# Attention with a gated MLP on one core: block 3 of the attention weights is copied to an fp32r tile, and its four transposes take fp32r operands

## The chip, the cores and the metric

The kernel runs on one core of a Trainium2 chip. The metric is the device time of one execution in microseconds. Before the change it is 828.13 us, the median of three runs (826.8 to 829.23).

## The reference

Eight batches with eight heads, 576 tokens, head size 64. For each head a causal attention with an extra bias from a running sum of `s`; the concatenated heads are the input `x` of a gated MLP that also mixes tokens. All in fp32.

```python
scores = scale * np.matmul(q, k.transpose(0, 1, 3, 2))
cum = np.cumsum(np.maximum(s, 0.0), axis=-1)
bias = -(cum[:, :, :, None] - cum[:, :, None, :])
scores = np.where(causal, -1000000000.0, scores + np.minimum(bias, 0.0))
attn = np.exp(scores - np.max(scores, axis=-1, keepdims=True))
attn = attn / (np.sum(attn, axis=-1, keepdims=True) + 1e-09)
o = np.matmul(attn, v)                       # then x = heads side by side
h = gelu(x @ w_in); u, v = halves of h
v_s = einsum('ts,bsd->btd', w_sg, layernorm(v) * g_ln) + b_sg
out = x + (u * v_s) @ w_out
```

## The kernel before

There are 64 heads (8 batches of 8), and after each 8 heads the MLP of that batch. A list of steps with due times (`POS`, in units of a head) sets the order in which the code issues them, with the MLP of batch b spread over the eight heads that come after it; a scheduler then orders the instructions of each engine from that list, and every engine runs its own list strictly in order. SyncE (SP) issues all transfers, from one queue.

**Precision.** Heads 0 to 7 use fp32 for scores, heads 0 to 11 for the product with the values (`NQ = 8`, `NP = 12`). From there on, operands are split in two fp32r tiles, a rounded part (hi) and the rest (lo), and a product is made of several fp32r matmuls that add up. In the code fp32r tiles are `F32R`; the profile prints fp32 and fp32r operands of a matmul alike as f32.

**A head**, in four generators that are advanced in turn:

- `split_head` splits keys and queries into `k1`, `k2`, and copies parts of them with transfers to `q1`, `q2` and back (L281 to L285).
- `scores` makes the scores of five blocks of query rows, `it` 0 to 4. Block 3 has 128 rows and 448 keys (`ITW`), block 0 has 64 rows and 64 keys. For each block VectorE adds the mask and takes the minimum of the negated scores (L305), which writes the block to `p`, ScalarE takes the exponential in place (L315). When all five are there, `norm` takes the reciprocals of the sums, and GpSimd multiplies each block in place (L338). Block 0 is not kept by itself: its normalised 64x64 values are written into columns 384 to 447, rows 0 to 63 of block 3, whose tile is 512 columns wide (`PW`). In the same way the second part of block 1 goes into block 2. So there are six operations on GpSimd per head from head 12 on. The `p` tiles exist twice (`pbuf`, by head parity), so a block of head h+2 can be written once block h has been read.
- `transposes` turns the blocks so that the keys stand on partitions: 13 transposes of 128x128 (one of them 64 columns) in four groups, each group in one bank of PSUM. A transpose is a matmul with the block's 128 columns as the loaded weights and the identity matrix `ident` as the moving operand (L377). Block 3 has four of the 13: columns 0 to 127 in the first group, 128 to 383 in the second, 384 to 511 in the fourth. After each group ScalarE and VectorE split the bank into hi and lo.
- `pv` multiplies with the values.

Weights, masks and the identity are made or loaded at the start, on VectorE and GpSimd, beside the running sums of `s`.

Of the kernel before, what the change touches and what calls it, by code (L numbers as in the profile page):

```python
# [8 lines left out]
F32 = mybir.dt.float32  # L9
F32R = mybir.dt.float32r  # L10
# [10 lines left out]
P = 128  # L21
# [16 lines left out]
PW = [64, 192, 384, 512, 576]  # L38
# [9 lines left out]
NP = 12  # L48
# [11 lines left out]
def tile_attn_gmlp(  # L60
# [12 lines left out]
    nc = tc.nc  # L73

    const = ctx.enter_context(tc.tile_pool(name="const", bufs=1))
    att = ctx.enter_context(tc.tile_pool(name="att", bufs=2))
# [6 lines left out]
    def eng(key):  # L83
        return [{"s": nc.scalar, "g": nc.gpsimd, "v": nc.vector}[x] for x in ENG[key]]

    def split(hi, lo, src, eng_hi, eng_lo):
        if eng_hi is nc.scalar:
            nc.scalar.copy(out=hi, in_=src)  # L88
        elif eng_hi is nc.gpsimd:
            nc.gpsimd.tensor_scalar(out=hi, in0=src, scalar1=1.0, scalar2=1.0, op0=ALU.mult, op1=ALU.mult)  # L90
        else:
            nc.vector.tensor_copy(out=hi, in_=src)
        eng_lo.tensor_tensor(out=lo, in0=src, in1=hi.bitcast(F32), op=ALU.subtract)  # L93

    heads = {}
# [41 lines left out]
    for c0, n in ((0, 512), (512, REM)):  # L137
        ps = ps_sc.tile([P, 512], F32, name="cps", tag="sc")
# [10 lines left out]
    for i in range(WARM):  # L149
# [7 lines left out]
    ident = const.tile([P, P], F32, name="ident")  # L157
    nc.vector.memset(ident, 0.0)
    nc.gpsimd.affine_select(out=ident, in_=ident, pattern=[[1, P]], base=0, channel_multiplier=-1,
                            compare_op=ALU.not_equal, fill=1.0)  # L160
    mask = const.tile([P, 448], BF16, name="mask")
    nc.vector.memset(mask, 0.0)
    nc.gpsimd.affine_select(out=mask, in_=mask, pattern=[[-1, 448]], base=320, channel_multiplier=1,
# [12 lines left out]
    pbuf = []  # L176
# [141 lines left out]
    def norm(h, its, rs):  # L318
        c = slice(min(its), max(its) + 1)
        nc.scalar.activation(out=rs[:, c], in_=sums[h % 2][:, c], func=AF.Copy, bias=1e-9)  # L320
        nc.vector.reciprocal(out=rs[:, c], in_=rs[:, c])  # L321
        for it in its:
            r, w = ITR[it], ITW[it]
            p = pbuf[h % 2][it][0:r, 0:w]
            e = eng("n0" if h < NP else "n")[it]


            o = [(p, p, rs[0:r, it:it + 1])]
            if it == 0:
                o = [(pbuf[h % 2][3][0:64, 384:448], p, rs[0:64, 0:1])]  # L330
            elif it == 1:
                o = [(p[:, 0:P], p[:, 0:P], rs[:, 1:2]),
                     (pbuf[h % 2][2][64:P, 256:320], p[64:P, P:192], rs[64:P, 1:2])]
            for po, pi, f in o:
                if e is nc.scalar:
                    nc.scalar.activation(out=po, in_=pi, func=AF.Copy, scale=f)
                else:
                    e.tensor_scalar(out=po, in0=pi, scalar1=f, scalar2=1.0, op0=ALU.mult, op1=ALU.mult)  # L338

    def scores(h):  # L340
        d = heads[h]
        d["mn"] = att.tile([P, 5], F32, name="mn", tag="mn")
        t = ps_sc.tile([P, 512], F32, name="sc", tag="sc")
        qk_part(h, 3, t, 0, 0, 448)
        qk_part(h, 0, t, 448, 0, 64)
        ttr(h, 3, t, 0, 0, 448, True)
        exp_(h, 3)
        ttr(h, 0, t, 448, 0, 64, True)
        exp_(h, 0)
        yield 0.5  # L350
        t = ps_sc.tile([P, 512], F32, name="sc", tag="sc")
        qk_part(h, 2, t, 0, 0, 320)
        qk_part(h, 1, t, 320, 0, 192)
        ttr(h, 2, t, 0, 0, 320, True)
        exp_(h, 2)
        ttr(h, 1, t, 320, 0, 192, True)
        exp_(h, 1)
        yield 0.5
        t = ps_sc.tile([P, 512], F32, name="sc", tag="sc")
        qk_part(h, 4, t, 0, 0, CH)  # L360
        ttr(h, 4, t, 0, 0, CH, True)
        t = ps_sc.tile([P, 512], F32, name="sc", tag="sc")
        qk_part(h, 4, t, 0, CH, S)
        ttr(h, 4, t, 0, CH, S, False)
        exp_(h, 4)
        yield 0.6
        rs = att.tile([P, 5], F32, name="rs", tag="rs")
        norm(h, (3, 0, 2, 1, 4), rs)
        yield 0.1

    def transposes(h):
        d = heads[h]
        pb = pbuf[h % 2]
        pt = {}

        def tr(ps, c, it, jb, n=P):
            nc.tensor.transpose(out=ps[0:n, c:c + P], in_=pb[it][:, jb:jb + n], identity=ident)  # L377

        def new(name, w):
            if h < NP:  # L380
                x = "hl"[h % 2]
                pt[name] = (att.tile([P, w], F32, name=name + x, tag=name + x, bufs=1),)
            else:
                pt[name] = tuple(att.tile([P, w], F32R, name=name + x, tag=name + x, bufs=1) for x in "hl")

        def evac(name, c0, ps, w, e=nc.scalar):
            if h < NP:
                o = pt[name][0][:, c0:c0 + w]
                (e.copy if e is nc.scalar else e.tensor_copy)(out=o, in_=ps[:, 0:w])  # L389
            else:  # L390
                hi, lo = (t[:, c0:c0 + w] for t in pt[name])
                split(hi, lo, ps[:, 0:w], nc.scalar, nc.vector)

        d["pt"] = pt
        t = ps_pt.tile([P, 512], F32, name="pt", tag="pt")
        for c, it in ((128, 3), (384, 2), (0, 1), (256, 4)):
            tr(t, c, it, 0)
        new("pa", 512)
        evac("pa", 0, t, 512)
        yield 0.43  # L400
        t = ps_pt.tile([P, 512], F32, name="pt", tag="pt")
        tr(t, 384, 3, 128)
        tr(t, 0, 3, 256)
        tr(t, 256, 2, 256)
        tr(t, 128, 4, 256)
        new("pb", 768)
        evac("pb", 0, t, 512, nc.vector)
        yield 0.43
        t = ps_pt.tile([P, 512], F32, name="pt", tag="pt")
        tr(t, 128, 2, 128)  # L410
        tr(t, 0, 4, 128)
        evac("pb", 512, t, 256)
        yield 0.43
        t = ps_pt.tile([P, 512], F32, name="pt", tag="pt")
        tr(t, 0, 4, 512, 64)
        tr(t, 64, 3, 384)
        tr(t, 192, 4, 384)
        if h < NP:
            pt["pd"] = (att.tile([P, 320], F32, name="pdh", tag="pdh", bufs=1),)
            nc.vector.tensor_copy(out=pt["pd"][0][0:64, 0:64], in_=t[0:64, 0:64])  # L420
            nc.vector.tensor_copy(out=pt["pd"][0][:, 64:320], in_=t[:, 64:320])
        else:
            hi, lo = pt["pd"] = tuple(att.tile([P, w], F32R, name="pd" + x, tag="pd" + x, bufs=1)
                                      for x, w in (("h", 320), ("l", 192)))
            nc.scalar.copy(out=hi[0:64, 0:128], in_=t[0:64, 0:128])
            nc.scalar.copy(out=hi[:, 128:320], in_=t[:, 128:320])
            nc.vector.tensor_tensor(out=hi[64:128, 0:128], in0=t[0:64, 0:128], in1=hi[0:64, 0:128].bitcast(F32),
                                    op=ALU.subtract)
            nc.vector.tensor_tensor(out=lo, in0=t[:, 128:320], in1=hi[:, 128:320].bitcast(F32), op=ALU.subtract)
        yield 0.35  # L430
# [294 lines left out]
```

## Time and profile before

| what | value |
|---|---|
| three runs | 826.8, 828.13, 829.23 us |
| span of the profiled execution | 828.8 us |
| transposes | 832, of which 208 of block 3 in heads 12 to 63 |
| bytes moved by DMA | 89.29 MB |

The profile is of one execution: its span goes from the first to the last instruction. PE is TensorE's matmul row and PEld its weight loads, which run beside it; DVE is VectorE, ACT ScalarE, POOL GpSimd, SP SyncE. A row of a group names line, engine, operation, output and inputs. The shape before the tile sizes (128*128) is rows times columns of the loaded weights, and the last (128x512) is that of the moving operand. A row of waits says who waited for whom: in all, how many times, the longest. Matmuls are pipelined, so the durations of neighbours overlap, and a rate is read from how one follows another.

### The profile page before, as it was taken

The page shows a single profiled execution, that of the slowest core. Times are in us where ns is not written, and L with a number is a line of the kernel's source. Part 1 is how long each engine was busy: PE and PEld are TensorE (multiplying, and loading weights), DVE is VectorE, ACT ScalarE, POOL GpSimd, SP SyncE. Part 2 cuts the span into 40 slices and gives each one's busy share as a digit, 9 for nine tenths or more (in the row PEclk, how much of TensorE's full clock was granted, in tenths as well). Part 3 has the DMA queues.
Part 4 walks back from the last instruction along what each step waited for, and adds up shares of the span by engine and source line. Part 5 has one row for each costly group of instructions (what it writes and reads, how often), then busy time and mean ns, then how long its engine had stood idle before and what let it go on. Part 6 is the DMA issues. An engine that isn't in the chain of part 4 may idle for free.

```text
span 828.8 us, 16733 instructions
## 1 busy us (share of the span) xinstructions
PE 792.6 (96%) x5161; PEld 696.1 (84%) x5161; DVE 597.9 (72%) x1806; ACT 576.5 (70%) x1620; POOL 595.1 (72%) x979
## 2 busy tenths in 40 slices
PE   6899999899999999999989999999999999999878
PEld 3355666889989998999979998899989998899778
DVE  5995468975787578966888577965888678963652
ACT  4787778775686678866878577866787677862430
POOL 4987668878677768796768778785778778872451
PEclk9999999999999999999999999999999999999989
DMA  7656553343442543444434453443444353400101
GB/s 210 215 158 181 148 139 84 86 105 100 116 106 74 128 125 86 108 121 126 112 82 104 115 139 90 113 109 96 119 119 103 100 152 93 98 26 23 35 8 57
DMA packets 69804, 89.29 MB, mean 108 GB/s; under 512 B 25954, under 2 KB 42212, under 8 KB 69716
## 3 DMA queue, kind: packets, MB, share of 16 engines
q1 hardware_dynamic: 69716, 88.23, 40.8%
q8 instruction: 41, 0.67, 0.4%
q14 instruction: 47, 0.39, 0.2%
HBM read 42.27 MB, written 9.73 MB: 63 GB/s over the span
## 4 chain that ended last, share of the span: by engine, by line
PE 73%; DVE 12%; DMA 5%; ACT 3%; issue 3%; POOL 2%; SPq 1%; DVEq 0%; POOLq 0%; ACTq 0%
PE om L616 12%; PE sm L597 11%; PE um L582 10%; PE xx L450 10%; PE vm L518 9%; PE pt L377 8%; PE sc L297 4%; PE sc L298 4%; DVE p L305 2%; DMA xq<-xs 2%; DMA q<-k 2%; PE sm L601 1%; PE sm L600 1%; DVE wbits L220 1%; DVE vm L504 1%
## 5 line engine op out<-in xcount | busy, mean ns | idle before, releaser
L338 POOL TENSOR_SCALAR p<-p,rs 128x448 f32<-128x448 f32 (+4 forms) x372 | 180.5, 499 | 29.1 <-DVE rs L321 9.6
L315 ACT ACTIVATE p<-p,mn 128x448 f32<-128x448 f32 (+4 forms) x320 | 177.9, 557 | 24.5 <-DVE mn L305 22.4
L305 DVE CUSTOM_DVE_ANT_0 p<-sc,mask 64x64 f32<-64x64 f32 (+4 forms) x320 | 126.2, 422 | 56.4 <-PE pt L377 31.0
L377 PE MATMUL pt<-ident,p 128*128 128x128 f32 (+1 forms) x832 | 137.2, 278 | 5.3 <-DVE pbl L389 2.6
L597 PE MATMUL sm<-ws,vn 128*128 128x288 f32 x768 | 130.3, 304 | 0.7 <-POOL vn L567 0.6
L93 POOL TENSOR_TENSOR k<-raw,k 128x576 fp32r<-128x576 f32 x56 | 80.3, 1433 | 66.7 <-ACT k L88 33.3
L582 PE MATMUL um<-xs,wi 128*128 128x288 f32 x768 | 123.4, 300 | 2.5 <-DVE u L504 2.4
L616 PE MATMUL om<-gt,wo 128*128 128x288 f32 x768 | 125.7, 298 | 0.0
L582 PEld LDWEIGHTS um<-xs,wi 128*128 128x128 f32 x768 | 108.9, 188 | 8.9 <-DVE u L504 4.0
L597 PEld LDWEIGHTS sm<-ws,vn 128*128 128x128 f32 x768 | 112.4, 192 | 3.3 <-DVE u L504 1.0
L377 PEld LDWEIGHTS pt<-ident,p 128*128 128x128 f32 (+1 forms) x832 | 96.8, 138 | 21.8 <-DVE pbl L389 5.4
L616 PEld LDWEIGHTS om<-gt,wo 128*128 128x128 f32 x768 | 110.6, 188 | 2.3
L518 PE MATMUL vm<-wi,xs 128*128 128x512 f32 x384 | 103.4, 399 | 0.0
L297 PE MATMUL sc<-k,q 128*128 128x448 f32 x336 | 100.8, 308 | 1.5 <-DVE mn L305 0.8
L298 PE MATMUL sc<-k,q 66*128 66x448 f32 x336 | 89.3, 298 | 0.6 <-DMA k<-cum 0.6
L88 ACT CAST pbh<-pt 128x512 fp32r<-128x512 f32 x104 | 48.9, 479 | 58.8 <-PE pt L377 58.8
L518 PEld LDWEIGHTS vm<-wi,xs 128*128 128x128 f32 x384 | 69.7, 189 | 14.9 <-POOL xs L93 1.6
L93 POOL TENSOR_TENSOR gt<-u,gt 128x288 fp32r<-128x288 f32 x64 | 50.7, 806 | 41.6 <-ACT gt L88 41.1
L297 PEld LDWEIGHTS sc<-k,q 128*128 128x128 f32 x336 | 60.8, 181 | 9.1 <-DVE mn L305 3.9
L93 DVE TENSOR_TENSOR pbl<-pt,pbh 128x512 fp32r<-128x512 f32 x104 | 56.5, 549 | 15.9 <-ACT pbh L88 15.9
L298 PEld LDWEIGHTS sc<-k,q 66*128 66x128 f32 x336 | 60.9, 181 | 5.9 <-issue 0.9
L88 ACT CAST k<-raw 128x576 fp32r<-128x576 f32 x56 | 37.6, 671 | 39.5 <-PE sc L297 33.8
(142 smaller groups left out, 1704.8 us busy)
## 6 DMA issues: line engine op xcount, KB each, us to landing
q<-k SPq DMA_DIRECT2D x168, 144.0 KB
raw<-in_kq SPq DMA_DIRECT2D x56, 288.0 KB
vr<-in_vp SPq DMA_DIRECT2D x52, 192.0 KB
out_t<-ot SPq DMA_DIRECT2D x64, 144.0 KB
k<-k SPq DMA_DIRECT2D x56, 144.0 KB
wraw<-in_w_in SPq DMA_DIRECT2D x16, 256.0 KB
kf<-in_kq SPq DMA_DIRECT2D x8, 288.0 KB
qf<-in_kq SPq DMA_DIRECT2D x8, 288.0 KB
```

The source lines that it names most:

```text
L88: nc.scalar.copy(out=hi, in_=src)
L93: eng_lo.tensor_tensor(out=lo, in0=src, in1=hi.bitcast(F32), op=ALU.subtract)
L297: nc.tensor.matmul(o, d["q1"][:, i0:i0 + r], d["k1"][:, j0:j1], start=True, stop=False)
L298: nc.tensor.matmul(o, q2[h % 2][:, i0:i0 + r], d["k2"][0:66, j0:j1], start=False, stop=True)
L305: nc.vector.tensor_tensor_reduce(out=pbuf[h % 2][it][0:r, j0:j1], in0=pst[0:r, c0:c0 + j1 - j0], in1=(mask2 if it in (2, 4) else mask)[0:r ...
L315: nc.scalar.activation(out=p, in_=p, func=AF.Exp, bias=d["mn"][0:r, it:it + 1], scale=-1.0, accum_out=sums[h % 2][0:r, it:it + 1])
L338: e.tensor_scalar(out=po, in0=pi, scalar1=f, scalar2=1.0, op0=ALU.mult, op1=ALU.mult)
L377: nc.tensor.transpose(out=ps[0:n, c:c + P], in_=pb[it][:, jb:jb + n], identity=ident)
L518: nc.tensor.matmul(ps[0:r], xs[c][:, xi, ts_], wi[:, c, wj, fs], start=(n == 0), stop=(n == 11))
L582: nc.tensor.matmul(ps[:, 0:CH], wi[:, c, wj, dt * P:(dt + 1) * P], xs[c][:, xi, cs], start=(n == 0), stop=(n == 11))
L597: nc.tensor.matmul(ps[:, 0:CH], vn[j][:, vi, ds_], ws[:, j, wj, cs], start=(n == 0), stop=False)
L616: nc.tensor.matmul(ps[:, 0:CH], wo[:, c, wj, ms], gt[ch, c][:, gi, :], start=(n == 0), stop=(n == 11))
```

## The change

A second identity of type fp32r is made at the start. From head 12 on, when block 0 has been written into block 3, a transfer from SyncE copies the whole block-3 tile, 128 partitions of 512 columns, to a new tile `r3` of type fp32r with two buffers. It moves bits, nothing is rounded in it. The four transposes of block 3 read `r3` and the fp32r identity, and write the bank through an fp32r view. The other nine stay as they were. The last line makes a scratch area in on-chip memory smaller, which frees room for the new tiles.

```diff
+    ident_r = const.tile([P, P], F32R, name="ident_r")
+    nc.vector.tensor_copy(out=ident_r, in_=ident)
...
+            if it == 0 and h >= NP:
+                d = heads[h]
+                d["r3"] = att.tile([P, PW[3]], F32R, name="r3", tag="r3")
+                nc.sync.dma_start(out=d["r3"].bitcast(F32), in_=pbuf[h % 2][3])
...
         def tr(ps, c, it, jb, n=P):
+            if it == 3 and h >= NP:
+                nc.tensor.transpose(out=ps[0:n, c:c + P].bitcast(F32R), in_=d["r3"][:, jb:jb + n], identity=ident_r)
+                return
             nc.tensor.transpose(out=ps[0:n, c:c + P], in_=pb[it][:, jb:jb + n], identity=ident)
...
-    nc = bacc.Bacc("TRN2", target_bir_lowering=False, num_devices=1)
+    nc = bacc.Bacc("TRN2", target_bir_lowering=False, num_devices=1, dynamic_dma_scratch_size=1024)
```

Up to head 11 the engines' lists stay as they were, but for the cast of the identity on VectorE, ahead of the first operation on `st`. From the first copy on, the scheduler orders all five engines anew. Three places show how. In the names, `p_0_3` is the tile of block 3 for even heads, `k1`, `k2`, `q1`, `q2` the parts of keys and queries, `xx` and `x0` the banks of the product with the values, `xs`, `gt` and `vs` tiles that are split for the MLP and the values; other numbers tell buffers apart. Lines of the new kernel stand 2 to 9 higher.

GpSimd at head 38, before: the six operations on `p`, and what stands among them.

```order
L338 TENSOR_SCALAR p_0_3_151<-p_0_3_151,rs_6267 128x448
L338 TENSOR_SCALAR p_0_2_149<-p_0_2_149,rs_6267 128x320
L338 TENSOR_SCALAR p_0_1_148<-p_0_1_148,rs_6267 128x128
L338 TENSOR_SCALAR p_0_4_153<-p_0_4_153,rs_6267 128x576
L93 TENSOR_TENSOR xs_6965<-xr_5519,xs_6965 128x576
L93 TENSOR_TENSOR gt_6541<-u2_5986,gt_6541 128x288
L338 TENSOR_SCALAR p_0_3_151<-p_0_0_147,rs_6267 64x64
L338 TENSOR_SCALAR p_0_2_149<-p_0_1_148,rs_6267 64x64
```

The same place now:

```order
L340 TENSOR_SCALAR p_0_3_153<-p_0_3_153,rs_6321 128x448
L340 TENSOR_SCALAR p_0_2_151<-p_0_2_151,rs_6321 128x320
L340 TENSOR_SCALAR p_0_1_150<-p_0_1_150,rs_6321 128x128
L340 TENSOR_SCALAR p_0_4_155<-p_0_4_155,rs_6321 128x576
L340 TENSOR_SCALAR p_0_3_153<-p_0_0_149,rs_6321 64x64
L340 TENSOR_SCALAR p_0_2_151<-p_0_1_150,rs_6321 64x64
L93 TENSOR_TENSOR vs_6271<-vr_6045,vs_6271 128x6x64
```

The two splits that stood ahead of block 0's write into block 3 no longer stand there.

TensorE at head 38, before: the end of the product with the values of the head ahead, and the first group of transposes.

```order
L472 MATMUL x0_6132<-pdh_6117,vs_6039 128x64
L450 MATMUL xx_6123<-pdl_6118,vs_6039 128x192
L450 MATMUL xx_6123<-pdh_6117,vs_6039 128x64
L377 MATMUL pt_6276<-ident_124,p_0_3_151 128x128
L377 MATMUL pt_6276<-ident_124,p_0_2_149 128x128
L377 MATMUL pt_6276<-ident_124,p_0_1_148 128x128
L377 MATMUL pt_6276<-ident_124,p_0_4_153 128x128
L297 MATMUL sc_6558<-k1_6544,q1_6546 128x448
```

The same place now:

```order
L481 MATMUL x0_6186<-pdh_6171,vs_6091 128x64
L625 MATMUL om_6691<-gt_6451,wo_170 128x288
L459 MATMUL xx_6177<-pdl_6172,vs_6091 128x192
L459 MATMUL xx_6177<-pdh_6171,vs_6091 128x64
L384 MATMUL pt_6332<-ident_r_129,r3_6326 128x128
L386 MATMUL pt_6332<-ident_124,p_0_2_151 128x128
L386 MATMUL pt_6332<-ident_124,p_0_1_150 128x128
L386 MATMUL pt_6332<-ident_124,p_0_4_155 128x128
L299 MATMUL sc_6625<-k1_6602,q1_6604 128x320
```

The group stays together, and block 3 comes first in it as before; what follows is another part of the scores, and from the last score of a head to its first transpose there are more matmuls than before (107 against 89 on average over heads 12 to 63).

SyncE at head 38, before: between the copies of keys and queries of two heads.

```order
L285 DMA k2_6367<-cum_78 2x576
L569 DMA vnr2_172<-vnr1_6162 64x512
L281 DMA q1_6546<-k1_6544 64x576
L282 DMA q2_0_145<-k1_6544 64x576
L115 DMA raw_6503<-in_kq 128x576
L283 DMA q1_6546<-k2_6545 64x576
```

The same place now:

```order
L287 DMA k2_6603<-cum_78 2x576
L578 DMA vnr2_174<-vnr1_6216 64x512
L344 DMA r3_6326<-p_0_3_153 128x512
L122 DMA vr_6223<-in_vp 128x384
L283 DMA q1_6761<-k1_6759 64x576
L284 DMA q2_1_158<-k1_6759 64x576
L115 DMA raw_6720<-in_kq 128x576
L285 DMA q1_6761<-k2_6760 64x576
```

The copy stands in the one queue, behind the transfers for the keys of one head and ahead of those of the next.

## The prediction

> **What bounds the kernel now.** I read the page first, for the share of each engine, then the table by stage, to see where TensorE is full, then the waits of TensorE inside the full stage, and last the groups by shape and a timeline, for what one transpose costs.
>
> The page: the span, and the busy time and share of each engine.
>
> ```profile
> span 828.8 us, 16733 instructions
> PE 792.6 (96%) x5161; PEld 696.1 (84%) x5161; DVE 597.9 (72%) x1806; ACT 576.5 (70%) x1620; POOL 595.1 (72%) x979
> ```
>
> The table by stage (busy time of each engine, granted clock, DMA share):
>
> ```profile
> 25.00:135.00 110.00, 104.23 (x489) 60.29 (x488) 77.37 (x255) 83.05 (x245) 83.58 (x132) 1.00 0.57 157
> 135.00:160.00 25.00, 22.85 (x140) 19.00 (x139) 23.03 (x65) 20.81 (x60) 21.51 (x34) 0.93 0.38 97
> 160.00:760.00 600.00, 591.17 (x4111) 552.01 (x4110) 450.28 (x1367) 440.24 (x1239) 452.21 (x741) 1.00 0.41 103
> 760.00:828.00 68.00, 58.94 (x380) 55.33 (x378) 31.44 (x67) 19.51 (x43) 23.57 (x48) 0.95 0.10 32
> ```
>
> From 160 to 760 us TensorE is busy for 591 of 600 us at full clock, while the other three compute engines stand at about 75%. That stage holds the split-precision heads, the only ones the change touches (heads 12 to 63, the first few of them before 160 us). There, a nanosecond less on TensorE is a nanosecond less of time, as long as nothing makes TensorE wait. The longest waits of TensorE in that stage, of its matmuls and then of its weight loads (total us, times, longest):
>
> ```profile
> PE vm L532 <- DMA xq<-xs: 2.9, 3, 1.8
> PE sc L297 <- DVE mn L305: 0.8, 2, 0.5
> ```
>
> ```profile
> PEld sc L297 <- DVE mn L305: 3.9, 11, 0.8
> PEld vm L532 <- DMA xq<-xs: 2.1, 1, 2.1
> ```
>
> They are short, and those for xq are for a transfer between two SBUF tiles, the kind of wait that the change adds.
>
> **The change part by part.**
>
> *What a transpose costs, and what it would cost.* First four fp32 transposes in a row on the timeline, then the groups by shape, matmuls and weight loads apart (behind the bar: busy us in all, mean ns of one, idle time before).
>
> ```profile
> 400.57 0.60 PE L377 MATMUL pt<-ident,p 128*128 128x128 f32 x4
> ```
>
> ```profile
> L377 PE MATMUL pt<-ident,p 128*128 128x128 f32 x768 | 130.3, 278 | 3.2 <-DVE xr L479 0.9 <-DVE pbl L389 0.8 <-ACT p L336 0.7
> L518 PE MATMUL vm<-wi,xs 128*128 128x512 f32 x384 | 103.4, 399 | 0.0
> L450 PE MATMUL xx<-pdh,vs 128*128 128x64 f32 x52 | 11.2, 215 | 0.0
> L450 PE MATMUL xx<-pdh,vf 128*64 128x192 f32 x24 | 6.5, 352 | 0.2 <-DVE pdh L421 0.2
> L450 PE MATMUL xx<-pah,vf 128*64 128x512 f32 x12 | 6.4, 618 | 0.0
> ```
>
> ```profile
> L377 PEld LDWEIGHTS pt<-ident,p 128*128 128x128 f32 x768 | 90.7, 140 | 13.1 <-ACT p L336 1.1 <-DVE xr L479 1.1 <-DVE pbl L389 1.0
> L297 PEld LDWEIGHTS sc<-k,q 128*128 128x128 f32 x280 | 53.1, 190 | 8.2 <-DVE mn L305 3.9 <-DVE pdh L421 2.0 <-DVE mv L548 0.5
> L295 PEld LDWEIGHTS sc<-kf,qf 128*128 128x128 f32 x80 | 13.3, 192 | 12.4 <-DVE mn L305 8.1 <-DVE pdh L421 1.5 <-DVE rs L321 0.5
> L297 PEld LDWEIGHTS sc<-k,q 128*64 128x64 f32 x56 | 7.7, 137 | 0.8
> L377 PEld LDWEIGHTS pt<-ident,p 128*64 128x64 f32 x64 | 7.0, 110 | 8.7 <-DVE pbl L389 4.3 <-DVE mn L305 1.6 <-ACT pbh L389 0.8
> ```
>
> The page prints fp32r matmul operands as f32 too; which is which follows from the code (vf, kf, qf are fp32, vs, wi, xs, k, q fp32r). Streaming, fp32: (618 - 352)/320 = 0.83 ns a column. Streaming, fp32r: (399 - 215)/448 = 0.41 ns. For the 128 columns of the identity that is 106 ns against 53. Four fp32 transposes take 0.60 us, so one follows another after (0.60 - 0.28)/3 = 0.107 us: the fp32 rate. Loading: an ordinary matmul needs (190 - 137)/64 = 0.83 ns a column, 106 ns for 128, with fp32r and fp32 alike (190 and 192); a transpose (140 - 110)/64 = 0.47, 60 ns. A load runs beside the stream of the matmul ahead, so each pair costs the longer of the two. I take the stream from the operand type (53) and the load from the kind of operation (60), since the load rows differ by operation and not by type. Then what follows an fp32r transpose comes 60 ns behind it instead of 107, a saving of 47 ns. In every head the four are followed by another transpose, as the order below shows for the first group. 52 heads x 4 = 208; 208 x 0.047 = 9.8 us.
>
> The other end for the load is the fp32r row, 106 ns. Then of the four successors three still save 47 ns, the second of the neighbouring pair saves nothing, and the first of a head, which stands behind a 64-column matmul (27 ns of stream), costs 46 more: 95 ns a head, 4.9 us. The Trainium skill, "TensorE: Matmul & The Clock Gate", section LDWEIGHTS, gives a load P/1.2 ns for P columns whatever the operand, 107 for 128, by which the sum would be this lower end; the rows of ordinary matmuls agree with it (106), those of the transposes do not (60).
>
> Four of the 52 heads lie before 160 us, where TensorE has gaps anyway, so I count 48/52: **-9.0 us**.
>
> *The second identity.* One cast on VectorE, which the order puts ahead of the first operation on the gate input. Priced by the cast there:
>
> ```profile
> 4.73 0.49 DVE L92 CAST sp<-st 128x320 fp32r<-128x320 f32 x1
> ```
>
> 128/320 of 0.49 is **+0.2 us**; everything at the start waits for that chain, so it is not hidden.
>
> *The copy.* 52 transfers of 256 KB from SyncE are 13.6 MB, over 600 us 23 GB/s beside the 103 GB/s and the DMA share of 0.41 in the table: bandwidth is there. What counts is the delay. The copy takes the whole tile, so also the columns 384 to 447 that the normalised block 0 is written into. Before, the first transposes of block 3 read other columns and needed only the first of the six normalisations on GpSimd. Now all four wait for the write of block 0, the fifth of the six, and then for the landing. How long a copy takes, by SyncE's timeline (issues) and by the chain that ended last:
>
> ```profile
> 410.58 0.54 SPq L282 DMA_DIRECT2D q<-k  x1
> 411.52 0.34 SPq L115 DMA_DIRECT2D raw<-in_kq  x1
> 411.90 0.46 SPq L283 DMA_DIRECT2D q<-k  x1
> 413.10 0.46 SPq L284 DMA_DIRECT2D k<-k  x1
> ```
>
> ```profile
> 411.90 3.79 DMA q<-k
> ```
>
> L284 overwrites what L282 reads, so 410.58 to 413.10 bounds a 144 KB copy at 2.5 us; the one queued behind the 288 KB load took 3.79. I take 3.8 for 256 KB. Against it stands the time from the write of block 0 to the first transpose. It differs by head; two ends, on the timeline: GpSimd and TensorE of head 34, then GpSimd and TensorE of head 38.
>
> ```profile
> 402.38 0.73 POOL L338 TENSOR_SCALAR p<-p,rs 64x64 f32<-64x64 f32 x2
> 410.69 0.65 PE L377 MATMUL pt<-ident,p 128*128 128x128 f32 x4
> ```
>
> ```profile
> 456.79 1.44 POOL L93 TENSOR_TENSOR xs<-xr,xs 128x576 fp32r<-128x576 f32 x1
> 458.19 0.81 POOL L93 TENSOR_TENSOR gt<-u,gt 128x288 fp32r<-128x288 f32 x1
> 458.97 0.73 POOL L338 TENSOR_SCALAR p<-p,rs 64x64 f32<-64x64 f32 x2
> ```
>
> ```profile
> 458.71 0.66 PE L377 MATMUL pt<-ident,p 128*128 128x128 f32 x4
> ```
>
> The first of the two small writes is block 0, done halfway through the 0.73 us. Head 34: done at 402.75, transposed from 410.69, 7.9 us of cover. Head 38: done at 459.33, transposed from 458.71, 0.6 us too early. Left in that order, head 38 would stall for 4.4 us. But the order moves: on GpSimd the two splits between the normalisations and block 0 (1.44 + 0.81 us) now stand behind it, and on TensorE, counted in the order over heads 12 to 63, 107 matmuls stand between a head's last score and its first transpose where 89 stood. 18 x 0.12 us (288 columns at 0.41 ns) is 2.2 us. -0.6 + 2.25 + 2.2 = 3.85 us against 3.8: covered, with nothing to spare, where it was worst. Work recurs every eight heads, so some six heads are like 38. I give each half of what TensorE waits per batch for xq, (2.9 + 2.1)/6 = 0.8: 6 x 0.4 = **+2.4 us**. The bounds are 0 and the second rival.
>
> Behind the copy SyncE holds the key and query copies of the head after next; the scores that need them do not show among TensorE's long waits above, and their place stays a whole head ahead.
>
> *What is released earlier.* The buffer of block 3 is free after the copy instead of after the fourth transpose group. VectorE waits for that from 160 to 760 us:
>
> ```profile
> DVE p L305 <- PE pt L377: 23.6, 31, 3.1
> ```
>
> But VectorE is busy for 450 of 600 us and TensorE waits on it at L297 for only 4.7 us (3.9 + 0.8). I count 0; at best 4.7 us go.
>
> **Sum**, against the profiled span of 828.8, which lies within the three runs (826.8 to 829.2, median 828.1): -9.0 + 0.2 + 2.4 = -6.4, so 828.1 - 6.4 = **821.7 us**.
>
> **The rivals.**
>
> *A transpose keeps its pace whatever the type* (the change doesn't do what it says). For it: load times already go by operation, and the 107 ns may be the pace of the mode and fit the fp32 rate by chance; no row shows an fp32r transpose. Against it: the fit is close, 107 and 106. Then nothing is saved and +0.2 + 2.4 remain: 830.7 us. The Trainium skill, "TensorE: Matmul & The Clock Gate", section "PE-mode transpose", says that the array's full clock does not engage for transposes, and gives 275 ns for a two-byte one in a kernel; by that, a narrower operand would not help. The trace agrees in the duration (278 ns, but with four-byte data) and not in the clock, granted at 1.00 from 160 to 760 us.
>
> *The copy is late at every head.* TensorE takes its instructions in order, so a transpose that is not ready stops everything behind it. A head saves 4 x 0.047 = 0.19 us; a mean wait above that makes the kernel slower, which is little beside a landing of 2.5 to 3.8. For it: xq, also an SBUF copy from SyncE, costs 0.8 us a batch, and in the new SyncE queue the copy stands behind transfers that wait themselves. Against it: the new order moves both ends apart by some 4 us, and the key copies, which are placed the same way, are not among TensorE's long waits. At 0.4 us in each of 48 heads: 19.2 - 9.0 + 0.2 = +10.4, 838.5 us.
>
> **How the numbers follow.** The forecast gets 0.56, the pace that stays 0.20, the late copy 0.24. The forecast's own range: best 9.8 saved and VectorE's 4.7 gone, 813.6; worst 4.9 saved and 4 lost at heads, about 828. The range that holds 8 in 10 reaches past 830.7 and a mean wait of 0.35 us a head: 814 to 836. A difference of 0.3% (2.5 us, about the spread of the three runs) is what can be told from no change. Faster: 0.50 of the first case and a little of the third, 0.53. Same: the forecast's upper end and half of the second, 0.17. Slower: 0.30.
>
> **What would show it.** Right: fp32r transposes with a mean near 220 ns and 60 ns apart, their loads at 140 ns; hardly a wait of TensorE for r3; 160 to 760 us shorter by 6 to 9 us. The pace that stays: 278 ns and 107 apart. The lower end: loads of 190 ns. The late copy: a row of TensorE at the block-3 transposes waiting for the r3 transfer, over 9 us in total. I am wrong altogether if TensorE's waits grow at other lines, since the order of all engines is new from head 12 on.

## The result, and the profile after

| kernel | median of the runs | to before (95% interval) |
|---|---|---|
| before | 828.13 us (826.8 to 829.23) | 1 |
| changed | 848.47 us (847.51 to 851.85) | 1.0258 (1.0226 to 1.0291) |

The change makes the kernel 20 us slower. The profiled execution took 851.85 us. Its page first, span and engines, then the stages by window.

```profile
span 850.1 us, 16949 instructions
PE 800.5 (94%) x5161; PEld 697.0 (82%) x5161; DVE 600.2 (71%) x1807; ACT 582.4 (69%) x1620; POOL 598.0 (70%) x979
```

```profile
25.00:135.00 110.00, 104.86 (x481) 60.89 (x481) 76.40 (x248) 81.77 (x239) 83.76 (x128) 0.97 0.56 152
135.00:160.00 25.00, 22.93 (x144) 18.02 (x142) 23.15 (x71) 22.26 (x65) 22.77 (x39) 1.00 0.49 138
160.00:760.00 600.00, 575.64 (x3951) 531.53 (x3951) 444.58 (x1352) 439.89 (x1224) 445.35 (x729) 0.99 0.46 124
```

The number to read is the count of matmuls between 160 and 760 us: x3951, where before had x4111. All in all there are as many matmuls as before (x5161 in both). In the same 600 us TensorE does 160 fewer; at before's pace, 600/4111 = 0.146 us each, that is 23 us. No other engine is fuller than it was (444.6, 439.9, 445.4 against 450.3, 440.2, 452.2), so none has become the bound. The count is read in the same way in the experiments below.

Next, the transposes. Two rows by tile (min/median/max in ns, matmuls and weight loads), the row of the group with its mean (behind the bar: busy us in all, mean ns of one), and a second group of a head on the timeline:

```profile
L384 PE MATMUL pt<-ident_r,r x208: 218/278/455, 143.3 to 778.5; 128*128 128x128 f32 x104
```

```profile
L384 PEld LDWEIGHTS pt<-ident_r,r x208: 137/140/224, 143.3 to 778.5; 128*128 128x128 f32 x104
```

```profile
L384 PE MATMUL pt<-ident_r,r 128*128 128x128 f32 x208 | 46.3, 264 | 2.3 <-DVE xr L488 1.5 <-DMA r<-p 0.8
```

```profile
402.98 0.29 PE L384 MATMUL pt<-ident_r,r 128*128 128x128 f32 x2
403.11 0.41 PE L386 MATMUL pt<-ident,p 128*128 128x128 f32 x2
```

Two fp32r transposes in a row take 0.29 us together and one of them at least 0.218, so the second starts at most 0.07 us after the first, and the next fp32 one 0.13 us after the first. Before it was 0.107 from one to the next. So inside the pair the forecast pace is there, and the loads have 140 ns, as forecast. The mean duration is not as forecast: 264 ns, where 220 was named for the right case and 278 for the pace that stays. What the pace is worth is measured by e7.

Then what TensorE waits for between 160 and 760 us, matmuls and then loads. Where a matmul and its load wait for the same thing, both rows count one and the same moment, so the two lists must not be added:

```profile
PE sm L610 <- DMA vnr<-vnr: 4.3, 3, 2.0
PE xx L459 <- ACT pah L88: 4.2, 5, 1.0
PE um L591 <- DVE vt L565: 2.9, 4, 0.9
PE xx L459 <- ACT pbh L88: 2.6, 9, 0.6
...
PE pt L384 <- DMA r<-p: 0.8, 2, 0.6
```

```profile
PEld xx L459 <- ACT pah L88: 5.5, 6, 1.2
PEld xx L459 <- ACT pbh L88: 5.4, 9, 0.9
PEld sm L610 <- DMA vnr<-vnr: 5.2, 4, 2.3
PEld sc L299 <- DVE mn L307: 4.5, 9, 0.8
PEld um L591 <- DVE vt L565: 3.8, 4, 1.2
```

TensorE waits for the copy itself for 0.8 us in all. It waits at other lines: for ScalarE's split of the transposed weights (`pah`, `pbh`), for a transfer of the MLP (`vnr`), for VectorE's step of the layer norm (`vt`). None of these instructions was changed; they stand in another order. This is the case that the prediction named last and gave no chance of its own. In all TensorE idles for 24.4 of the 600 us, where it idled for 8.8 before.

A smaller part of the loss is in the granted clock (third figure from the end, 0.99 against 1.00). Behind some of the pauses it falls to half for about 3.4 us. Here is one case, in three windows of 3.4 us, the first with TensorE idle for 1.65 us:

```profile
362.00:365.40 3.40, 1.75 (x11) 1.07 (x10) 3.05 (x6) 3.08 (x8) 3.23 (x6) 1.00 0.51 143
365.40:368.80 3.40, 3.40 (x15) 3.10 (x14) 3.40 (x12) 1.83 (x6) 1.33 (x3) 0.50 0.21 59
368.80:372.20 3.40, 3.40 (x27) 3.37 (x27) 0.61 (x2) 0.99 (x4) 2.18 (x4) 1.00 0.00 0
```

The changed kernel's trace has five such stretches from 160 to 760 us, that of the kernel before has one. At half the clock 3.4 us cost at most 1.7, so the four more are at most 7 of the 23 us.

### The profile page after: what moved, and what is told of

It reads as the page before. It is cut to its first block, busy times and chain, and to the rows that moved or that the text cites. A ratio compares the mean times of both kernels' runs of the same rounds, so it can differ in the third digit from the quotient of the medians.

```text
span 850.1 us, 16949 instructions
## 1 busy us (share of the span) xinstructions
PE 800.5 (94%) x5161; PEld 697.0 (82%) x5161; DVE 600.2 (71%) x1807; ACT 582.4 (69%) x1620; POOL 598.0 (70%) x979
## 4 chain that ended last, share of the span: by engine, by line
PE 61%; DVE 11%; ACT 10%; DMA 7%; POOL 5%; issue 5%; SPq 0%; DVEq 0%; POOLq 0%; ACTq 0%
PE om L625 11%; PE sm L606 9%; PE vm L527 8%; PE um L591 8%; PE xx L459 7%; PE pt L386 5%; PE sc L300 4%; PE sc L299 3%; ACT p L317 3%; DVE p L307 2%; DMA q<-k 2%; POOL p L340 2%; PE sm L610 1%; DMA r<-p 1%; PE pt L384 1%
## 5 line engine op out<-in xcount | busy, mean ns | idle before, releaser
L307 DVE CUSTOM_DVE_ANT_0 p<-sc,mask 128x448 f32<-128x448 f32 (+4 forms) x320 | 122.8, 422 | 51.9 <-PE pt L386 23.9
L625 PE MATMUL om<-gt,wo 128*128 128x288 f32 x768 | 123.6, 298 | 0.6 <-DVE u L513 0.4
L386 PE MATMUL pt<-ident,p 128*128 128x128 f32 (+1 forms) x624 | 118.8, 284 | 4.8 <-DVE pbl L398 2.1
L386 PEld LDWEIGHTS pt<-ident,p 128*128 128x128 f32 (+1 forms) x624 | 71.7, 140 | 19.9 <-DVE pbl L398 4.9
L93 POOL TENSOR_TENSOR vs<-vr,vs 128x384 fp32r<-128x384 f32 x52 | 53.7, 1033 | 15.0 <-DMA q<-k 6.6
```

What stands on the lines that cost most here:

```text
L307: nc.vector.tensor_tensor_reduce(out=pbuf[h % 2][it][0:r, j0:j1], in0=pst[0:r, c0:c0 + j1 - j0], in1=(mask2 if it in (2, 4) else mask)[0:r ...
L625: nc.tensor.matmul(ps[:, 0:CH], wo[:, c, wj, ms], gt[ch, c][:, gi, :], start=(n == 0), stop=(n == 11))
```

## The experiments

Three theories. **A**: the new order of all engines costs, because the scheduler has to plan around a copy at every head. **B**: the copy costs on the chip, by its place in SyncE's queue, by VectorE's wait to overwrite block 3, or by its landing. **C**: any new order costs, since the old one was a good one and a plan is a throw of dice.

Some kernels below take their instructions in the order of another kernel. For that, each engine's list is read from the other program, and every instruction gets an order-only dependency on the one ahead of it in that list:

```diff
         tile_attn_gmlp(tc, *args)
+        force_order(tc)
...
+        for a, b in zip(perm, perm[1:]):
+            tc.add_manual_dep(mine[b + 0], mine[a].name, how, reason="order")
```

"Old order" is that of the kernel before, "new order" that of the changed kernel. Every ratio is to the kernel before, run beside it. Forcing an order costs little by itself: e7 and e8 are forced and no slower than before.

### The copy without a reader, without the pace, and the pace without the copy

**e1**, the copies are made and nobody reads them:

```diff
-            if it == 3 and h >= NP:
-                nc.tensor.transpose(out=ps[0:n, c:c + P].bitcast(F32R), in_=d["r3"][:, jb:jb + n], identity=ident_r)
-                return
```

> The 52 copies of block 3 are made as in the changed kernel, but nobody reads them: all 13 transposes of a head read p in fp32, as before. The instructions of TensorE, VectorE, ScalarE and GpSimd stand in the same order as in the kernel before (but for the cast of the second identity), and SyncE's list is that of before with the copies put in. So this run holds what the copies do on the chip by themselves: their place in SyncE's queue, where the copy waits for GpSimd and holds up what is behind it, their bandwidth, and VectorE's wait to overwrite block 3's tile. Theory A (the new order of all engines is what costs, the copy itself is cheap): 828 to 832 us. Theory B (the copy on the chip costs, by SyncE's queue or by VectorE's wait for the landing): 840 to 856 us, the 848.5 of the changed kernel plus up to the 6.6 us that the pace of the transposes saves there.

Measured: 828.15 us, 1.0023 (1.0009 to 1.0036). SyncE does wait at the copy for GpSimd:

```profile
SPq L344 <- POOL p L340: 43.5, 32, 6.1
```

43.5 us of SyncE's waiting cost the kernel 1.9 us. As long as the old order stands and nobody reads the copies, two parts of B, the queue and VectorE's wait, have almost nothing. The third, TensorE's wait for the landing, comes in e5.

**e2**, the copy read as fp32 (`r3` typed `F32`, `identity=ident`):

> The copy is made and read, but r3 is typed fp32 and its four transposes take fp32 operands: the copy without the pace. The order of the engines is a third one. If the order of the changed kernel costs what it costs because the transposes now wait for a copy in the plan (theory A in its systematic form), and the pace saves 6.6 us (worked out from the trace of the changed kernel), this kernel takes 848.5 + 6.6 = 855 us, within 4 us. If each new order is a throw of dice of its own (theory C: the plan is sensitive, and any change of it moves the time by some per cent either way), it may land anywhere from 830 to 860. If the pace saves nothing (the rival that the change does not do what it says), 848 us.

Measured: 847.31 us, 1.0264 (1.0231 to 1.0297). As slow as the changed kernel, with no fp32r transpose in it, and 8 us under the 855 of A in its systematic form. It lies at the 848 of "the pace saves nothing" too; e7 decides that.

**e3**, no transfer; GpSimd writes block 3 to an fp32r tile:

```diff
+            if it == 3 and h >= NP:
+                o = [(rbuf[h % 2][:, 0:448], p, rs[:, 3:4])]
```

> The pace without the copy: GpSimd's normalisation of block 3 writes straight into a fp32r tile (two of them, in turn), and the four transposes read it as fp32r; there is no transfer. Block 3's weights are therefore rounded to fp32r here, which the copy did not do. Theory B (the copy on the chip costs): the copy's costs are gone and 6.6 us are saved, 820 to 823 us. Theory A in its systematic form (planning around a copy is what costs): also 820 to 823, since no copy is planned; it parts from B in e1. Theory C (any new order costs, or is a throw of dice): 830 us or more is possible. If the pace saves nothing: 828.

Measured: 839.84 us, 1.0163 (1.0134 to 1.0191). Without any copy, and with the pace, 13 us slower than before. This speaks against B and against A in its systematic form.

**e4**, the changed kernel with three buffers for block 3 (`h % 3` in place of `h % 2`):

> The changed kernel with three buffers in turn for block 3 of the weights in place of two, so that VectorE does not wait for the landing of head h's copy before it writes block 3 of head h+2 (it writes the third tile). Theory B with VectorE's wait as the main cost: most of the 20 us go, 825 to 835 us. Theory B with SyncE's queue as the main cost, or theory A: 843 to 850, as the transposes still wait for the copy and the queue stays as it is. The order of the engines changes here too, so theory C allows 830 to 855.

Measured: 844.08 us, 1.0223 (1.0197 to 1.0249). VectorE no longer waits for the landing of the copy, and 18 of the 20 us are still there. (The order is a new one here too.)

### Order and change taken apart

**e5**, all of the change in the old order:

> The changed kernel's instructions, all of them, but every engine is made to take them in the order of the kernel before (SyncE with the copies where e1 has them, TensorE with fp32r transposes from r3 where the fp32 ones stood). Nothing is planned around the copy, so this shows what TensorE would wait for it in the old order. From e1's trace, start of the copy's issue against the first transpose of each head: with 2.3 us to land, the transposes of heads 16, 30, 38, 46, 54 and 62 would come 1.5 to 4.9 us too early and TensorE would wait 19 us from head 16 on; with 3.8 us, 35 us. Less 6.6 us for the pace, from e1's 828: 840 (landing 2.3) to 856 us (landing 3.8), with a row of TensorE's waits at the fp32r transposes for the transfer. The prediction's term for this was 2.4 us; if that was right for the old order, 824 us.

Measured: 862.91 us, 1.0471 (1.0432 to 1.0509). The matmul waits from 160 to 760 us:

```profile
PE pt L384 <- DMA r<-p: 18.7, 6, 4.9
PE vm L541 <- DMA xq<-xs: 2.3, 3, 1.3
```

And the first of them from 135 to 800 us:

```profile
PE pt L384 <- DMA r<-p: 25.6, 9, 4.9
```

Six heads stall for the copy in the full stage, 3 us each, the longest 4.9; there are two more stalls before it and one behind it. The time is 7 us over the upper end that was expected. 25.6 - 4.8 + 1.9 = 23 of the 37 us are the stalls, the pace (e7) and the copies (e1). The other 14 can be the granted clock, which falls to half behind these stalls as in the case above. The window shows 0.98, where e7's below shows 1.00:

```profile
160.00:760.00 600.00, 569.91 (x3922) 529.80 (x3922) 436.80 (x1337) 429.12 (x1212) 437.49 (x722) 0.98 0.45 123
```

Over the whole span the mean clock is 0.976 of 859.4 us, and in e1 0.994 of 827.5. So 20.6 against 5.0 us of clock are missing, at most 15.6 us more; how much of that the kernel lost was not measured apart.

**e6**, the new order without the change (and with a third buffer for block 3):

> The order of the changed kernel on all five engines, without the change: no copies, all transposes fp32 from p. Block 3 has three buffers here, since with two the order would not be free of deadlock without the copy. Theory A (the new order is what costs): 848 to 857 us, the changed kernel's 848.5 plus up to 6.6 us for the pace that is missing here, less what its transfers cost. Theory B (the copy on the chip costs): 828 to 834 us.

Measured: 849.7 us, 1.0293 (1.0251 to 1.0334). The window, the longest waits of TensorE's loads in it, and of its matmuls the one for `vnr`:

```profile
160.00:760.00 600.00, 581.22 (x3959) 537.84 (x3958) 443.07 (x1343) 439.65 (x1221) 445.58 (x731) 0.99 0.39 102
```

```profile
PEld xx L458 <- ACT pbh L88: 6.4, 9, 1.6
PEld xx L458 <- ACT pah L88: 5.0, 5, 1.2
PEld sc L306 <- DVE mn L314: 4.1, 9, 0.6
PEld um L590 <- DVE vt L564: 3.4, 4, 1.0
PEld pt L385 <- DVE pal L93: 3.2, 7, 0.5
PEld sm L609 <- DMA vnr<-vnr: 2.0, 3, 1.1
```

```profile
PE sm L609 <- DMA vnr<-vnr: 1.3, 3, 0.8
```

No copy, no fp32r transpose, and x3959 matmuls, almost the changed kernel's x3951. The waits for `pbh`, `pah`, `mn` and `vt` are the same ones too. The order by itself costs 24 us (0.0293 of 825; interval 21 to 28), the half-clock stretches behind its pauses included. Only the wait for `vnr` is clearly shorter than with the copies: 2.0 against 5.2 us for the loads, 1.3 against 4.3 for the matmuls, so 3 us. That the copies delay this transfer is not shown: it is one trace of each kernel, and e9 below, with no copy at all, waits for it as long as the changed kernel does:

```profile
PEld sm L604 <- DMA vnr<-vnr: 5.5, 5, 2.8
```

**e7**, the pace alone, e3 in the old order:

> The pace alone in the old order: no copy, GpSimd writes the normalised block 3 into a fp32r tile (its weights are rounded to fp32r by that), the four transposes read it as fp32r, and every engine takes its instructions in the order of the kernel before. If e3's 839.8 us (the same work in an order of its own) came from its order: 819 to 822 us, before less 6.6 us. If the faster transposes bring nothing because another engine or a buffer sets the pace: 826 to 829. If e3's time came from GpSimd's write into a second tile: 838 to 840.

Measured: 820.39 us, 0.9942 (0.9921 to 0.9964).

```profile
160.00:760.00 600.00, 593.51 (x4159) 552.77 (x4159) 450.65 (x1369) 438.83 (x1239) 452.49 (x740) 1.00 0.40 104
```

48 matmuls ahead of before, 7.0 us by the trace; by the timed runs 4.8 us (3.0 to 6.5). The same work in an order of its own (e3) was 18 us slower (0.0163 + 0.0058 of 826). This pair has the same instructions in two orders and nothing else.

**e8**, the change in the old order, the copy in two transfers:

```diff
-            if it == 0 and h >= NP:
+            if it in (3, 0) and h >= NP:
...
+                cs = slice(0, 384) if it == 3 else slice(384, 512)
+                nc.sync.dma_start(out=d["r3"].bitcast(F32)[:, cs], in_=pbuf[h % 2][3][:, cs])
```

> As e5 (the change, in the old order on all engines), but the copy goes in two transfers: columns 0 to 383 as soon as GpSimd has normalised block 3, columns 384 to 511 after block 0 has been written into them; only the transpose of the fourth group needs the second. From e1's trace the first part then starts 2 to 4 us earlier at the heads that wait in e5 (head 38: 11.7 us after its first score operation, landing by 15.5 with 3.8 us, and the transposes from 16.0). If e5's waits are the landing of a late copy, nearly all of them go: 822 to 826 us. If the copy on the chip costs in another way (its place in SyncE's queue, 52 more transfers): 830 us or more.

Measured: 823.49 us, 0.9988 (0.9967 to 1.001). The stalls of e5 are gone with the earlier start. What held e5 up was that the copy waited for block 0, not that it was a copy. (Its first transfer is also smaller, 192 KB in place of 256.)

### How good the old order is

**e9** and **e10**, the kernel before with one tiny operation on GpSimd, at head 12 or at head 13:

```diff
         norm(h, (3, 0, 2, 1, 4), rs)
+        if h == 12:
+            nc.gpsimd.tensor_scalar(out=scrap, in0=rs[:, 0:1], scalar1=1.0, scalar2=1.0, op0=ALU.mult, op1=ALU.mult)
```

> The kernel before with one tiny operation more: at head 12 GpSimd multiplies 128x1 values into a scrap tile that nobody reads. It costs well under 1 us by itself, but the scheduler's order is another one from there on (of TensorE's 5043 instructions 4447 still stand in the same order, of VectorE's 1808 1528). It tells why the new order is bad. If any new plan from head 12 on loses what the old one had (theory C, a plan is a throw of dice and the old one a good throw): 835 to 850 us. If the old order is nothing special, and the plan is worse only where it plans around a copy (theory A, systematic): 825 to 830.

> The same one operation at head 13 in place of 12, a second throw: the order is again another (TensorE 4454 of 5043, VectorE 1548 of 1808 in the old order). Theory C: between 825 and 850 us, and not the same as e9. Theory A: 825 to 830.

Measured: 835.28 us, 1.0097 (1.0064 to 1.013), and 834.62 us, 1.0095 (1.0078 to 1.0112). The operation in e9 by tile, and two windows of e9 and then of before:

```profile
L371 POOL TENSOR_SCALAR scrap<-rs x1: 194/194/194, 137.7 to 137.7; 128x1 f32<-128x1 f32 x1
```

```profile
135.00:400.00 265.00, 255.54 (x1744) 236.81 (x1744) 194.52 (x585) 190.32 (x531) 198.28 (x318) 0.98 0.38 101
400.00:760.00 360.00, 356.02 (x2471) 330.98 (x2469) 278.64 (x847) 272.00 (x764) 275.66 (x457) 1.00 0.39 104
```

```profile
135.00:400.00 265.00, 259.99 (x1798) 241.47 (x1797) 200.94 (x610) 195.52 (x555) 203.45 (x325) 0.99 0.42 107
400.00:760.00 360.00, 354.03 (x2453) 329.54 (x2452) 272.37 (x822) 265.53 (x745) 270.26 (x450) 1.00 0.40 100
```

0.19 us of work on an engine that is not full costs 8 us. All of it is lost before 400 us (54 matmuls fewer, 8 us). Behind that the order of e9 is the old one again, and it is as fast (x2471 against x2453). Theory C was expected to part e9 from e10; the two are alike.

**e13**, that operation at each head from 12 on (`if h >= 12`). **e14**, the kernel before with one due time moved (`f1=9.7` in place of 9.6). **e15**, the changed kernel with `f1=9.5`. **e16**, the split copy of e8 in the scheduler's own order, with `f0=2.3, f1=10.0`.

> The kernel before with the tiny GpSimd operation of e9 (0.19 us there) at each of the heads 12 to 63. No copy, no fp32r transposes. TensorE's order between one batch and the next agrees to 0.37, 0.45 and 0.50 (share of instructions in the same sequence, heads 24 to 31 against 32 to 39 and so on), where the kernel before has 0.99, 1.00 and 1.00 and the changed kernel 0.75, 0.65 and 0.58. If anything that recurs keeps the plan from repeating, and that is what costs: 840 to 852 us. If the plan around a copy is what costs: 832 to 837, about as the single operation.

> The kernel before with one number changed: the end of a batch's MLP is due at 9.7 heads in place of 9.6. Nothing is added. Its order does not repeat (0.30, 0.48, 0.44). If the lack of a repeating order costs: 838 to 850 us. If a plan without the copy is good whatever its order: 826 to 832.

> The changed kernel with the end of a batch's MLP due at 9.5 heads in place of 9.6. Its order nearly repeats (0.91, 0.98, 0.98). If the lack of a repeating order was the cost: 824 to 834 us. If planning around the copy costs whatever the order's rhythm: 842 to 850.

> The copy in two transfers as in e8, but planned by the scheduler itself, with the MLP due from 2.3 to 10.0 heads in place of 2.0 to 9.6. Its order repeats (0.99, 1.00, 0.93), in a rhythm that is not that of the kernel before. If a repeating order is enough: 822 to 830 us, like e8's 823.5 in the old order. If the old order was a good one besides: 835 to 850.

Measured: e13 842.69 us, 1.0155 (1.0125 to 1.0186); e14 846.57 us, 1.0183 (1.0139 to 1.0226); e15 856.09 us, 1.0319 (1.0273 to 1.0365); e16 834.77 us, 1.0065 (1.004 to 1.0091). The windows of e14 and of e15, and e15's loads:

```profile
160.00:760.00 600.00, 579.39 (x3989) 538.15 (x3988) 446.85 (x1351) 437.04 (x1226) 443.70 (x731) 0.99 0.40 102
```

```profile
160.00:760.00 600.00, 573.74 (x3917) 529.57 (x3917) 441.21 (x1341) 440.73 (x1215) 442.63 (x725) 0.98 0.46 124
```

```profile
PEld xx L459 <- ACT pah L88: 7.8, 7, 1.2
PEld sm L610 <- DMA vnr<-vnr: 5.8, 5, 2.5
PEld um L591 <- DVE vt L565: 5.8, 5, 1.2
```

e14 has nothing of the change in it, only a number that is 0.1 higher, and it is 122 matmuls behind (18 us). That is theory C, and A is not needed: an order needs no copy in it to be bad. Nor is it mainly the clock, which stands at 0.99 in this window, and at 1.00 in that of e13 (x4029, 82 matmuls behind). My further idea, that repeating from batch to batch is what makes an order good, falls with e15. Its order nearly repeats, and it is worse than the changed kernel: the same three waits come back 5 to 7 times, about once a batch. The order of e16 repeats as well, in another rhythm, and its time lies between the two cases that were expected: 6 us slower than the same split copy in the old order (e8). What makes the old order good stays open. What was found is that each of the ten other orders that the scheduler made cost something: e3 18 us against e7, e16 6 against e8, and e2, e4, e6, e9, e10, e13, e14 and e15 8 to 26 us against before (e2, e4 and e15 with the copies in them).

### The rest of the sum

**e11**, e8 with GpSimd issuing its transfers itself (`nc.gpsimd.dma_start`):

> As e8 (two transfers, old order on all engines), but GpSimd itself issues them, each right behind the operation that wrote its columns, so nothing in SyncE's queue waits for GpSimd. If what parts e8 (823.5) from e7 (820.4) is SyncE's queue, which holds up the transfers behind the copy: 820 to 822 us. If it is the copies' share of the transfer engines, or the landing: 823 to 825. If issuing costs GpSimd much of its own time, and it is in order too: more than 826.

Measured: 858.82 us, 1.0389 (1.0368 to 1.0411). The issues among GpSimd's groups:

```profile
L346 POOL DMA_DIRECT2D r<-p x104 | 63.0, 606 | 41.5 <-POOL p L340 41.5
```

Each issue holds GpSimd for 606 ns, and it waits 41.5 us more for its own writes ahead of them. That is 105 us on an engine that works in order, and what stands behind the issues comes later. Which of these delays makes the 32 us is not shown.

**e12**, e7 with block 4 in an fp32r tile too, so 9 of 13 transposes:

> As e7 (pace alone, old order, no copy), but block 4 of the weights is written to a fp32r tile as well, so that 9 of a head's 13 transposes take fp32r operands (blocks 3 and 4 are rounded to fp32r by that). If each fp32r transpose saves TensorE time that the kernel gets in full: e7's 5 us times 9/4, so 11 us below before, 813 to 816 us. If a load of about 82 ns between neighbouring fp32r transposes or another engine sets a floor: 817 to 821, little better than e7.

Measured: 822.78 us, 0.995 (0.9934 to 0.9967). No better than four of 13. From the first load of a group to the load behind it, median over the heads, the first, second and fourth group took 389, 462 and 351 ns before, 362, 392 and 302 in e7, and 363, 391 and 305 in e12. The third, with no transpose of block 3 and one of block 4, took 240 in e7 and 243 in e12. So by the medians 146 ns per head are saved (52 heads: 7.6 us) and the other five give nothing.

**e17**, e8 with the copies at other places in SyncE's queue, and **e18**, with the first of the two alone:

> As e8 (the copy in two transfers, the old order on PE, VectorE, ScalarE and GpSimd), but their places in SyncE's queue are chosen from the trace of e7: each stands ahead of the first transfer that e7 issued after GpSimd had written the columns, so that SyncE hardly waits at a copy. If the 3 us between e7 and e8 are the queue: 820 to 822 us, ratio to before 0.993 to 0.996. If they are the transfers themselves: as e8, 823 to 825, ratio 0.997 to 1.000.

> As e17, but only columns 0 to 383 are copied, so there is one transfer of 192 KB per head, and the transpose of columns 384 to 511 stays fp32 and reads p. Three quarters of the fp32r transposes; by the sequences of the changed kernel's trace 93 of 139 ns per head are kept, 3.3 us of e7's 5.0. If transfers cost by their number: about as e17, 821 to 824. If the pace decides: 1 to 2 us slower than e17.

Measured: 825.38 us, 0.9978 (0.9961 to 0.9995), and 826.22 us, 0.9993 (0.997 to 1.0016). The two ways to place the copies can't be told apart, nor can half as many transfers. e17 is the change at its best here with nothing rounded: 0.2% faster than before and 2.7% faster than the changed kernel. e7 is faster still, but it rounds block 3.

## Why the prediction was wrong

**The pace**, -9.0 us: right in its sign, too large in its size. e7 measured -4.8 (3.0 to 6.5), its trace -7.0. The forecast had 47 ns behind each of the four. In the groups (e12's numbers) the fourth, with one of them, saved 49; the second, with two side by side, 70 of 94; the first, where fp32r leads, 27 of 47: 146 of 188 ns per head. Why the five more of e12 brought nothing, also where fp32 ones stand ahead of them, stays open. By the Trainium skill, "TensorE: Matmul & The Clock Gate", section LDWEIGHTS, the load goes by its number of columns, which gave the lower end of 4.9 us. e7 agrees with that time, but by the number alone: the lower end has the three groups save 1, 47 and 47 ns, and they saved 27, 70 and 49. The load rows do not agree with the rule either: 140 ns for a transpose in fp32r as in fp32, against 190 for an ordinary matmul. Of the rivals, the pace that stays is excluded by e7.

**The second identity**, +0.2 us: not measured apart; it is in e1's +1.9.

**The copy**, +2.4 us, by the cover of the new order: right in the mechanism. TensorE waits 0.8 us for it. (The price was too high: the 2.9 and 2.1 us for `xq` that it adds up hold the same wait of 1.8 us, seen once from the matmul and once from its load.) The other half was right too: "Left in that order, head 38 would stall for 4.4 us" and "some six heads are like 38" are e5's 6 waits of up to 4.9. SyncE's queue was taken as harmless. That holds in the old order (e1); in the new one TensorE waits 3 us longer for `vnr` than in e6, and whether the copies do that is not shown.

**What is released earlier**, 0: right. Nothing of the 4.7 us went: TensorE's loads wait 4.5 us for VectorE's `mn` at the scores, 3.9 before.

**The step that failed** is the one that let the order in: "But the order moves: on GpSimd the two splits ... now stand behind it, and on TensorE ... 107 matmuls stand between a head's last score and its first transpose where 89 stood". It booked the 3.85 us of cover that the new order gives and booked nothing for the rest of that order, although the lists of all five engines were new from head 12 on. The sum treated a new order as neutral. It costs 24 us (e6), in pauses of TensorE at lines that the change does not touch and in the half clock behind some of them. With it the sum closes: -4.8 (e7) + 1.9 (e1) + 24.2 (e6) = +21, and +20 was measured. That it closes to 1 us is partly luck, as e6 alone is known to 3 or 4.

**The late copy**, the rival on the slow side, came nearest in time (838.5) and was wrong in its mechanism: it needs a wait at r3 of 0.4 us in every head, 19 us, and there were 0.8. In the old order (e5), where the scheduler had not moved things out of the copy's way, its sum of waits did come, 18.7 us, but at six heads and not at every one. The range up to 836 was worked out from these cases alone; none of them had a price for the order.

## What to carry to other kernels

Where a scheduler places the instructions, a change has two prices: that of its own operations, and that of the new order. The second can be the larger one by far, even for an edit of 0.2 us, and it can be measured by itself by running the new order without the change, or the change in the old order. A change that seems to fail should be tried in the old order before it is given up: here the same idea, with its copy split, went from 2.6% slower to 0.2% faster (0.05% to 0.4%).

## What was not expected

- One operation of 0.19 us on GpSimd, at one head of 64, made the kernel 8 us slower (e9, e10).
- A queue that waits 43.5 us at the copies cost 1.9 us (e1), so what stood behind them was hardly needed sooner.
- A pause of TensorE can cost more than itself: behind some pauses the granted clock stood at 0.50 for 3.4 us, as in the windows shown.
- The saving from fp32r transposes does not grow with their number: 4 of 13 give 0.9942, 9 of 13 give 0.995.
- Issuing a transfer from GpSimd takes 606 ns of that engine (e11). The issues of SyncE shown in the prediction take 0.34 to 0.54 us, on an engine with nothing else to do.
